# K and Q rounded in the second layer's quanta, loads six pairs ahead, joined visits from the ninth pair on

## The chip, the cores and the metric

One core of one Trainium2 chip. The metric is device time in microseconds (us) of one execution. A core has five engines that run their own instruction queues in order and wait for each other through semaphores: TensorE (PE, with its weight loads PEld), VectorE (DVE), ScalarE (ACT), GpSimd (POOL) and SyncE (SP, which here only issues transfers).

## The reference

Attention with a window of 32 positions to each side and 8 global positions, over 8 batches x 8 heads x 576 positions x 64; then a two-layer network on the 4608 tokens of width 512.

```python
scores = scale * np.matmul(q, k.transpose(0, 1, 3, 2))
mask = np.abs(pos[:, None] - pos[None, :]) <= window
mask = mask | is_global[:, None] | is_global[None, :]
scores = np.where(mask, scores, -1000000000.0)
attn = softmax(scores)
x = np.matmul(attn, v)            # heads side by side: 4608 x 512
h = x @ w_in                      # 512 -> 2048
r = np.maximum(h, 0.0)
g = s * (r * r) + b
out = g @ w_out                   # 2048 -> 512
```

## The kernel before, in words

**Pairs.** Two heads of one batch are a pair; there are 32, four to a batch. A pair's scores come in two halves, g = 0 and 1, each a call of `qk(p, g)` (line 623): six matmuls of K's transposed tile `kt` against Q's transposed tile `qt` into PSUM (`pss`, or `psw` in the second pool), an exponential on ScalarE (`em`, line 641), and a multiplication with the mask on VectorE one slot later (line 642). `pvq` (line 644) multiplies the `em` halves of two pairs with V (`po`); `norm_steps` turns `po` into `xt`, the input of the network: `ln` and `rep` on ScalarE, `gs`, `tot`, `xg` and `xt` on VectorE. `scatter` copies the global rows with POOL.

**The network in quanta.** `moe_quanta` (line 738) is a generator over 9 tiles of 512 tokens. A tile has 16 quanta of the first layer (4 matmuls `psh`, then a relu `r` on ScalarE and, one slot later, its square `g` on VectorE) and 16 of the second (4 matmuls `pso` each; after four quanta VectorE stores 128 rows). Ahead of the first tile, `lead()` takes the first steps of it: halves of four quanta that need two heads only.

**Slots.** `run_pair` (line 856) gives each pair 8 slots s = 0..7. In a slot it issues the pieces of attention that a rule puts there, runs what the slot before left over (`prev`), then the list `extra` of the slot (filled by `at(s, f, ...)` in the loop of line 1111), and ends with `Q(nq[s])`, as a rule one quantum. The queues of all engines are written in this order. From pair 13 on the phase is steady: the second layer runs from slot 4 of a batch's last pair (hp = 3) to slot 3 of the next batch's second pair (hp = 1), the first layer from there on.

**Visits.** Up to pair 11 (`JOIN`) the two halves of a pair come at two slots of their own. From pair 11 on there is one visit in slot 3 (`VISIT`): `visit(p)` (line 847) computes the second half of pair p and the first half of pair p + 1 together; the latter uses two PSUM banks (`ps_w`, tile `psw`) that belong between visits to the ring `ps_n` of the network. `BANKS` says by the slot since the visit which of the two rings a quantum's bank comes from. For pair 11 itself the rules of both kinds hold: the first half in slot 0, the visit in slot 3, and in slot 4 the unjoined second half.

**How K and Q get ready.** From pair 8 on, K is loaded by SP in float32 (`natk`, four slots, `load_nat`), rounded to bfloat16 by ScalarE (`round_k`, line 234, `natb`) and turned by a transposing transfer that SP issues (`turn_k`, line 293, tile `kt`, three buffers). `put_kq(p, (0,))` (line 546) then copies the 8 global columns into `kt` on VectorE (line 552). Q is loaded (`load_q`, `natq`) and rounded (`round_q`, line 276, `sixq`); up to pair 17 TensorE transposes it (`trans_b`, `pst`) and VectorE takes it out, from pair 18 (`QTURN`) on `turn_q` does; `put_kq(p, (1,))` copies its global columns. SP's queue holds the loads of K, Q and V (V up to pair 15; later POOL) and the transposes, in the order of the program, and a transfer waits for the landing of the eighth before it.

**When.** The loop of line 1111 sets the slots: loads of K and Q five pairs ahead; the roundings of two pairs in each last and each first pair of a batch (`todo`, lines 1160 to 1174, slots 1, 3, 5 and 7); `turn_k(p + 2)` at the start of a pair; `put_kq(p + 1, (0,))` in slot 2 (line 1132), one slot before the visit.

Of the kernel before, what the change touches and what calls it, by code (L numbers as in the profile page):

```python
# [40 lines left out]
NSIX = 8  # L41
NSIXQ = 13
JOIN = 11
# [3 lines left out]
VISIT = 3  # L47
BANKS = "mmnnmnmm"
# [36 lines left out]
def kernel(  # L85
# [471 lines left out]
    def trans(t, p):  # L557
        if p < 5 or (t == "k" and p > 5):
            ps = bank("pst").bitcast(BF16)[:, 0:LQ]
        elif t == "k" or p == JOIN + 1:  # L560
# [41 lines left out]
    def trans_b(p, later=later):  # L602
        ps = trans("q", p)

        def evac():
# [12 lines left out]
            if p >= 6:  # L618
                put_kq(p, (1,) if p >= NSIX else (0, 1))
# [118 lines left out]
    def moe_quanta():  # L738
        for t in range(NTOK // 512):
# [116 lines left out]
    def run_pair(p, nq, extra):  # L856
# [4 lines left out]
        for s in range(8) if p > 4 else range(NCH, 8):  # L861
            prev, later[:] = list(later), []
            now = []
            joined = p > JOIN
            if p >= JOIN:
                when[0] = (s - VISIT) % 8
# [6 lines left out]
            if joined and s in (4, 5):  # L873
                step()
                if s == 5 and hp == 0:
                    later.append(lambda: scatter(bi - 1))
            if s < NCH:
                if s in (2, 3) and not joined:
                    step()
                if s == 4 and hp == 0 and bi > 1 and not joined:  # L880
# [16 lines left out]
            elif s == 5:  # L897
                if p == 4:
                    cast_v(A, 5)
                if 4 < p < JOIN:  # L900
                    trans_b(p + 1, now)
            if s == 4 and 4 < p < NSIX - 1:
                trans_a(p + 1, now)
            if s in (5, 6) and not joined:
# [3 lines left out]
            if p > 4 and s == (VISIT if joined else 4 if p % 2 else 1):  # L908
# [157 lines left out]
    lead()  # L1066
    qk(4, 1)
# [43 lines left out]
    for p in range(4, NPAIR):  # L1111
# [13 lines left out]
        if p in (JOIN, JOIN + 1):  # L1125
            nq[(1, VISIT)[p - JOIN]] = 0
        if p > 7 and hp != 3 and p + 2 < NPAIR:
            turn_k(p + 2)
        if p >= JOIN and p + 1 < NPAIR:
            if p + 1 >= QTURN:  # L1130
                at(1, put_kq, p + 1, (1,))
            at(2, put_kq, p + 1, (0,))
        elif NSIX <= p + 1 < NPAIR:
            at(7, put_kq, p + 1, (0,))
        for j in {4: (8,), 5: (9,), 6: (10,), 7: (11, 12)}.get(p, (p + 5,)):
            if j < NPAIR:
                if j in (10, 11, 12):
# [110 lines left out]
```

## Time and profile before

| | us |
|---|---|
| median of three runs | 347.2 (345.22 to 347.98) |
| the profiled execution, its own time | 344.5 |
| its span, first to last instruction | 342.9 |
| PE busy in the span | 325.4 |
| DVE, ACT, POOL busy | 205.9, 201.0, 113.8 |
[...]

The profile follows one execution on the core. The busy time of an engine is the union of its instructions; idle time of TensorE is what lies between. A row of a timeline gives the start, the length, engine, line, operation, tile written <- tile read, shape, and in brackets the idle time of that engine before it and the instruction that ended it. Bank and buffer numbers are left out of the names.

### The profile page before, as it was taken

The numbers are of one execution on the slowest core, as the hardware profiler recorded it, in microseconds if no ns is written. First come the engines' busy times: TensorE is split into PE (matmuls) and PEld (weight loads), VectorE is DVE, ScalarE is ACT, GpSimd is POOL, SyncE is SP. The second block draws the span as 40 slices with busy tenths as digits, with TensorE's granted clock in tenths as the row PEclk, the third lists the DMA queues.
The fourth block names the chain that finished last, engine by engine and source line by source line (L and its number), as shares of the span: only waits on it lengthen the run. The fifth ranks groups of instructions, "written<-read, shape, count | busy, mean of one in ns | idle before, by whom it ended". The sixth has DMA issues, their size and how long they took to land.

```text
span 342.9 us, 8737 instructions
## 1 busy us (share of the span) xinstructions
PE 325.4 (95%) x3370; PEld 168.3 (49%) x3370; DVE 205.9 (60%) x541; ACT 201.0 (59%) x338; POOL 113.8 (33%) x220
## 2 busy tenths in 40 slices
PE   7898899899999999999899989998999999999995
PEld 4555343444444444477544444444466544444444
DVE  5489677555758688856665666566656534423422
ACT  3555787647795578567855885588358505503600
POOL 7741842143001415372368306831670030000000
PEclk9999999999999999999999999999999999999999
DMA  9999999989998999999499999993960011011012
GB/s 154 193 211 196 209 206 192 221 173 250 164 158 149 217 190 176 194 175 161 81 227 211 194 136 223 201 189 83 210 124 2 2 68 56 0 62 61 3 44 78
DMA packets 133533, 50.08 MB, mean 146 GB/s; under 512 B 122124, under 2 KB 128588, under 8 KB 133484
## 3 DMA queue, kind: packets, MB, share of 16 engines
q1 hardware_dynamic: 101346, 28.33, 48.7%
q0 software_dynamic: 31792, 20.77, 35.7%
q8 instruction: 26, 0.43, 0.5%
q10 hardware_dynamic: 354, 0.43, 0.4%
q14 instruction: 15, 0.12, 0.1%
HBM read 42.35 MB, written 9.44 MB: 151 GB/s over the span
## 4 chain that ended last, share of the span: by engine, by line
PE 73%; ACT 5%; DMA 5%; issue 5%; POOL 3%; SPq 3%; DVE 3%; POOLq 1%; ACTq 0%
PE pso L787 35%; PE psh L753 29%; PE po L658 5%; ACT r L775 3%; SPq L224 3%; DMA win_t<-in_moe_w_in_dram 2%; PE pss L634 2%; DVE g L778 2%; PE psw L634 1%; DMA natq<-in_q_dram 1%; DMA kt<-natb 1%; ACT em L641 1%; POOL sixq L197 1%; ACT sixq L278 1%; POOL gf L392 1%
## 5 line engine op out<-in xcount | busy, mean ns | idle before, releaser
L753 PE MATMUL psh<-xt,win_t 128*128 128x512 bf16 (+2 forms) x704 | 131.1, 341 | 1.0 <-POOL xt L730 0.6
L787 PE MATMUL pso<-wout_t,g 128*128 128x512 bf16 (+1 forms) x592 | 129.8, 374 | 0.0
L775 ACT ACTIVATE r<-psh 128x512 bf16<-128x512 f32 x144 | 85.1, 599 | 59.4 <-PE psh L753 58.8
L753 PEld LDWEIGHTS <-win_t 128*128 128x128 bf16 x704 | 63.4, 98 | 58.5 <-issue 2.1
L778 DVE TENSOR_TENSOR g<-r 128x512 bf16<-128x512 bf16 x144 | 60.4, 422 | 47.5 <-ACT r L775 46.1
L787 PEld LDWEIGHTS <-g 128*128 128x128 bf16 x592 | 55.9, 98 | 62.8
L641 ACT ACTIVATE em<-pss 128x840 bf16<-128x840 f32 (+1 forms) x42 | 37.3, 888 | 49.5 <-PE pss L634 49.4
L642 DVE TENSOR_TENSOR em<-em,mask 128x840 bf16<-128x840 bf16 (+1 forms) x65 | 39.2, 609 | 34.2 <-ACT em L641 33.9
L730 POOL COPY xt<-xg 128x4 bf16 (+1 forms) x72 | 16.8, 233 | 58.8 <-DVE xt L705 55.0
L807 DVE SCALAR_TENSOR_TENSOR osb<-pso,sb,bias_row 128x512 f32<-128x512 f32 (+1 forms) x25 | 18.2, 728 | 30.1 <-PE pso L787 30.0
L224 POOL DMA_DIRECT2D vring<-in_v_dram x33 | 29.5, 897 | 10.8 <-PE po L658 10.0
L705 DVE TENSOR_TENSOR xt<-po,rep 128x480 bf16<-128x480 f32 (+2 forms) x60 | 24.5, 449 | 2.1 <-ACT rep L715 2.1
L634 PEld LDWEIGHTS <-kt 64*128 64x128 bf16 x390 | 12.1, 99 | 26.4 <-issue 14.1
L811 POOL DMA_DIRECT2D out_dram<-osb x16 | 9.0, 565 | 32.1 <-DVE osb L807 25.3
L634 PE MATMUL pss<-qt,kt 64*128 64x192 bf16 (+4 forms) x252 | 16.1, 239 | 2.9 <-DVE qt L938 1.4
L641 ACT ACTIVATE em<-psw 128x904 bf16<-128x904 f32 x20 | 18.5, 926 | 0.0
L658 PE MATMUL po<-em,vring 128*32 128x160 bf16 (+3 forms) x840 | 17.7, 221 | 0.5 <-issue 0.5
L235 ACT CAST natb<-natk 128x640 bf16<-128x640 f32 x24 | 17.3, 722 | 0.5 <-DMA natk<-in_k_dram 0.5
L712 ACT ACTIVATE ln<-po 128x324 f32<-128x324 f32 (+1 forms) x30 | 12.9, 430 | 5.8 <-PE po L658 5.8
L715 ACT ACTIVATE rep<-ln 128x324 f32<-128x324 f32 (+1 forms) x32 | 14.7, 460 | 0.5
L658 PEld LDWEIGHTS <-vring 128*32 128x32 bf16 x896 | 13.7, 98 | 0.8 <-issue 0.8
L950 PE MATMUL psf<-dummy 128*128 128x512 bf16 x21 | 10.3, 573 | 1.8 <-DVE dummy L320 1.4
(125 smaller groups left out, 246.9 us busy)
## 6 DMA issues: line engine op xcount, KB each, us to landing
natk<-in_k_dram SPq DMA_DIRECT2D x47, 150.0 KB
natv<-in_v_dram SPq DMA_DIRECT2D x28, 150.0 KB
natq<-in_q_dram SPq DMA_DIRECT2D x55, 75.0 KB
wst<-in_moe_w_out_dram POOLq DMA_DIRECT2D x8, 512.0 KB, 5.0
out_dram<-osb POOLq DMA_DIRECT2D x16, 256.0 KB, 2.3
vring<-in_v_dram POOLq DMA_DIRECT2D x31, 75.0 KB, 5.3
out_dram<-osbh POOLq DMA_DIRECT2D x9, 256.0 KB, 2.8
win_t<-in_moe_w_in_dram POOLq DMA_DIRECT2D x4, 512.0 KB
```

What stands on the lines that cost most here:

```text
L224: eng.dma_start(out=dst[r : r + rows, n, c : c + nch, hh], in_=bass.AP(tensor=src[t].tensor, offset=o + c * KC * D, ap=[[D, rows], [KC * D ...
L235: nc.scalar.copy(out=natb[:, p % NV].rearrange("p (c h d) -> p c h d", c=NCH, h=2), in_=natk[:, p % NV],)
L634: nc.tensor.matmul(ps[:, hh, at : at + hi - lo], ktile[p][r, P * c : P * c + P], qbufs[p % 3][r, lo:hi], start=at == 0, stop=at + hi - lo ...
L641: nc.scalar.activation(em[:], ps[:, :, 0:n], AF.Exp, scale=SCALE)
L642: later.append(lambda: nc.vector.tensor_mul(em[:], em[:], masks[g]))
L658: nc.tensor.matmul(po[DH * j : DH * j + DH, a : a + n], view(vring[:, p % NVR, c, hh, part - 1 :], [2, DH]) if part else onesb[:], emt[(p, ...
L705: nc.vector.tensor_tensor(out=view(xt[:, 2 * g, x0 + t0 :], [NXT, 2], [w, runs], [1, w]), in0=view(po[:, STEP[blk] + col :], [STEP[blk], 2 ...
L753: nc.tensor.matmul(psh[:, d0 : d0 + n], win_t[:, a, f * P : f * P + P], xt[:, a, x0 : x0 + n], start=(a == 0 and j == 0), stop=(a == 3), s ...
L775: nc.scalar.activation(r[:], psh, AF.Relu)
L778: later.append(lambda g=g, r=r: nc.vector.tensor_mul(g[:], r[:], r[:]))
L787: nc.tensor.matmul(pso[:, 0:nn], gl[f][:, u * P : u * P + P], wout_t[:, f, n0 : n0 + nn], start=(f == 0), stop=(f == 15),)
L807: nc.vector.scalar_tensor_tensor(out=osb[:, 0:nn], in0=pso[:, 0:nn], scalar=s_bc, in1=bias_row[:, n0 : n0 + nn], op0=OP.mult, op1=OP.add,)
```

## The change

The table `VISITS` gives each visit's slot, counted over all pairs: slot 7 in pairs 8 and 9, 6 in pair 10, 5 in pair 11, 3 from pair 12 on. `JOIN` becomes 8, and at pair 8 only the first half is computed on its own. Everything that hung on slot 3 now hangs on the distance to a visit: the transposes of Q three slots ahead, the copies of the global columns two slots ahead, the normalization one and two slots behind, the bank of a quantum. The roundings, transposes and loads follow tables by pair.

```diff
-JOIN = 11
+JOIN = 8
-VISIT = 3
-BANKS = "mmnnmnmm"
+VISITS = {8 * p + {8: 7, 9: 7, 10: 6, 11: 5}.get(p, 3): p for p in range(JOIN, NPAIR)}
...
-            pool = rings[int(name == "psg" or BANKS[when[0]] == "n")]
+            ago = min((when[0] - x for x in VISITS if x <= when[0]), default=8)
+            left = min((x - when[0] for x in VISITS if x > when[0]), default=8)
+            near = ago < 2 or left < 3 or ago == 4
+            pool = rings[int(name == "psg" or not near)]
...
                     into(led[f], f, (0, 1))
-                    if f % 2:
-                        yield
+                    yield
...
-            if p >= JOIN and s == VISIT:
+            if at in VISITS:
                 visit(p)
-            elif not joined and p > 4 and s in ((0, 4) if p % 2 else (1, 3)):
+            elif 4 < p < JOIN and s in ((0, 4) if p % 2 else (1, 3)) or (p, s) == (JOIN, 1):
                 qk(p, int(s > 1))
-            if p >= JOIN and s == 0 and p + 1 < QTURN:
-                trans_b(p + 1, now)
+            j = VISITS.get(at + 3, NPAIR) + 1
+            if j < QTURN:
+                trans_b(j, now)
...
     qk(4, 0)
     lead()
+    lead()
     qk(4, 1)
...
+    k_out = turned(trans_a, 5)
+    lead()
     q_out = turned(trans_b, 5)
-    k_out = turned(trans_a, 5)
+    k_out()
     q_out()
-    k_out()
...
-        if p >= JOIN and p + 1 < NPAIR:
-            if p + 1 >= QTURN:
-                at(1, put_kq, p + 1, (1,))
-            at(2, put_kq, p + 1, (0,))
...
+        for s in range(8):
+            j = VISITS.get(8 * p + s + 2, NPAIR) + 1
+            if j < NPAIR:
+                at(s, put_kq, j, (0, 1) if j >= QTURN else (0,))
+        if p + 1 == NSIX:
+            at(7, put_kq, NSIX, (0, 1))
+        for j in range(p + 1, min(p + 7, NPAIR)):
+            x = {
+                10: (6, 1), 11: (7, 4), 12: (7, 5), 17: (12, 0), 18: (13, 0), 19: (14, 0),
+                20: (14, 4),
+            }.get(j, (j - 5 if j < 17 else j - 6, 0))
...
-            todo = {8: (11,), 9: (12,)}.get(
-                p, {0: (p + 3, p + 4), 3: (p + 2, p + 3)}.get(hp, ())
-            )
-            for i, j in enumerate(todo):
-                if j < NPAIR:
-                    x = 4 if p in (8, 9) else 4 * i
-                    at(1 + x, round_k, j)
...
+                d, k_at, q_at = ((4, 6, 7), (4, 0, 2), (3, 4, 6), (3, 0, 2))[j % 4]
+                k_at = {
+                    8: (6, 4), 9: (7, 1), 10: (7, 5), 11: (8, 5), 12: (9, 5), 13: (10, 5),
+                    17: (13, 6),
+                }.get(j, (j - d, k_at))
...
+                t_at = {
+                    8: (6, 5), 9: (7, 3), 10: (7, 7), 11: (8, 7), 12: (9, 7), 13: (10, 7),
+                    14: (11, 6),
+                }.get(j, (j - 3, 5))
...
         elif p == 7:
-            at(3, steps[1])
+            at(4, steps[1])
```

What the tables move is seen in the queues. ScalarE, the first-layer stretch at pair 19 (`r` relus, `natb` and `sixq` the roundings of pair 21, `em` the visit's two exponentials), before:

```order
L775 ACTIVATE r<-psh 128x512
L715 ACTIVATE rep<-ln 128x292
L775 ACTIVATE r<-psh 128x512 x4
L235 CAST natb<-natk 128x640
L278 CAST sixq<-natq 128x640
L775 ACTIVATE r<-psh 128x512 x2
L641 ACTIVATE em_3364<-pss 128x840
L641 ACTIVATE em_3377<-psw 128x904
```

and in the changed kernel at the same place:

```order
L777 ACTIVATE r<-psh 128x512
L718 ACTIVATE rep<-ln 128x292
L777 ACTIVATE r<-psh 128x512 x6
L644 ACTIVATE em_3387<-pss 128x840
L644 ACTIVATE em_3400<-psw 128x904
```

The two casts have left the stretch; they stand two pairs earlier, in the second layer, between two visits.

VectorE at the same place (`g` squares, `qt<-gqt` and `kt<-gkt` the copies of global columns for pair 20), before:

```order
L778 TENSOR_TENSOR g_3322<-r 128x512
L552 COPY qt_119<-gqt_120 128x5x8
L778 TENSOR_TENSOR g_3340<-r 128x512
L552 COPY kt<-gkt 128x5x8
L1107 TENSOR_TENSOR osbh<-osbh,bias_row 128x512
L778 TENSOR_TENSOR g_3356<-r 128x512
L642 TENSOR_TENSOR em_3364<-em_3364,mask_454 128x840
```

and changed:

```order
L780 TENSOR_TENSOR g_3347<-r 128x512
L554 COPY kt<-gkt 128x5x8
L554 COPY qt_119<-gqt_120 128x5x8
L780 TENSOR_TENSOR g_3364<-r 128x512
L1115 TENSOR_TENSOR osbh<-osbh,bias_row 128x512
L780 TENSOR_TENSOR g_3379<-r 128x512
L645 TENSOR_TENSOR em_3387<-em_3387,mask_454 128x840
```

The copy of `kt` has moved ahead of one square.

ScalarE at the visit of pair 11 (`em`: three halves before, of which the third repeats the first), before:

```order
L641 ACTIVATE em_2024<-pss 128x840
L641 ACTIVATE em_2037<-psw 128x904
L284 CAST sixq<-natq 120x640
L641 ACTIVATE em_2059<-pss 128x840
L310 CAST vring<-natv 128x640
```

and changed:

```order
L312 CAST vring<-natv 128x640
L237 CAST natb<-natk 128x640
L644 ACTIVATE em_2063<-pss 128x840
L644 ACTIVATE em_2076<-psw 128x904
L715 ACTIVATE ln<-po 128x324
```

One exponential less, and the casts of V stand ahead of the visit.

## Rows read from the trace of the kernel before

**Rows 1.** The page: busy us, share of the span and instructions of each engine.
```profile
PE 325.4 (95%) x3370; PEld 168.3 (49%) x3370; DVE 205.9 (60%) x541; ACT 201.0 (59%) x338; POOL 113.8 (33%) x220
```

**Rows 2.** Stretches: length, then PE, PEld, DVE, ACT, POOL busy (instructions), clock, DMA, GB/s.
```profile
66.00:104.80 38.80, 37.05 (x381) 17.49 (x377) 24.00 (x61) 26.82 (x45) 6.95 (x14) 1.00 1.07 186
104.80:260.00 155.20, 151.69 (x1679) 80.22 (x1682) 103.81 (x268) 104.63 (x178) 69.12 (x121) 1.00 1.10 172
```

**Rows 3.** Timeline of PE at the visit of pair 19.
```profile
164.44 0.35 PE L634 MATMUL pss<-qt,kt 64*128 64x92 bf16 x6
165.73 0.37 PE L634 MATMUL psw<-qt,kt 64*128 64x160 bf16 x6 [0.94 <-DVE kt L552]
```

**Rows 4.** Timeline of ACT ahead of the same visit.
```profile
163.29 0.72 ACT L235 CAST natb<-natk 128x640 bf16<-128x640 f32 x1
163.90 0.73 ACT L278 CAST sixq<-natq 128x640 bf16<-128x640 f32 x1
164.53 1.08 ACT L775 ACTIVATE r<-psh 128x512 bf16<-128x512 f32 x2
```

**Rows 5.** Timeline of DVE ahead of the same visit.
```profile
165.16 0.42 DVE L778 TENSOR_TENSOR g<-r 128x512 bf16<-128x512 bf16 x1 [1.22 <-ACT r L775]
165.50 0.17 DVE L552 COPY kt<-gkt 128x40 bf16<-128x40 bf16 x1
```

**Rows 6.** Groups, PE, 104.8 to 259 us: count | busy us, mean ns | idle before, releaser.
```profile
L634 PE MATMUL psw<-qt,kt 64*128 64x160 bf16 (+2 forms) x108 | 6.5, 227 | 3.4 <-DVE kt L552 3.2
```

**Rows 7.** Timeline of PE at pairs 11 and 12.
```profile
97.43 0.36 PE L634 MATMUL pss<-qt,kt 64*128 64x92 bf16 x6 [0.47 <-ACT em L641]
97.72 0.39 PE L658 MATMUL po<-em,onesb 128*32 128x160 bf16 x12
...
104.85 0.36 PE L634 MATMUL pss<-qt,kt 64*128 64x92 bf16 x6
...
105.34 0.37 PE L658 MATMUL po<-em,onesb 128*32 128x92 bf16 x12
```

**Rows 8.** Waits of PE, 66 to 104.8 us: us in total, times, longest.
```profile
PE pss L634 <- DVE kt L552: 0.6, 2, 0.4
...
PE psw L634 <- DVE kt L552: 0.2, 1, 0.2
```

**Rows 9.** The page's groups: weight loads of all halves of scores.
```profile
L634 PEld LDWEIGHTS <-kt 64*128 64x128 bf16 x390 | 12.1, 99 | 26.4 <-issue 14.1
```

**Rows 10.** Timeline of PE, pairs 7 and 8.
```profile
58.77 0.25 PE L514 MATMUL psg<-ident,gb 64*64 64x64 bf16 x4 [0.77 <-DVE gb L506]
...
61.90 0.42 PE L575 MATMUL pst<-ident,sixq 96*128 96x96 bf16 x6 [0.90 <-ACT em L641]
...
65.87 0.37 PE L634 MATMUL pss<-qt,kt 64*128 64x160 bf16 x6
...
66.85 1.90 PE L787 MATMUL pso<-wout_t,g 128*128 128x512 bf16 x8
68.68 0.36 PE L634 MATMUL pss<-qt,kt 64*128 64x92 bf16 x6
68.97 1.25 PE L787 MATMUL pso<-wout_t,g 128*128 128x512 bf16 x5
```

**Rows 11.** Timeline of SP's queue: issues of loads and transposing transfers.
```profile
44.65 4.03 SPq L264 DMA_DIRECT2D natq<-in_q_dram  x1
...
61.48 2.78 SPq L295 DMA_TRANSPOSE kt<-natb  x2
...
98.21 3.11 SPq L295 DMA_TRANSPOSE kt<-natb  x1
...
137.94 1.35 SPq L224 DMA_DIRECT2D natk<-in_k_dram  x2
```

**Rows 12.** Timeline of DVE at the copy for pair 8.
```profile
65.43 0.39 DVE L552 COPY kt<-gkt 128x40 bf16<-128x40 bf16 x1 [0.16 <-DMA kt<-natb]
```

**Rows 13.** Timeline of PE near the end: one second layer without attention.
```profile
297.62 13.98 PE L787 MATMUL pso<-wout_t,g 128*128 128x512 bf16 x64
```

More of the change, by code (lines that the diff above doesn't have):

```diff
@@ L559, in trans @@
             ps = bank("pst").bitcast(BF16)[:, 0:LQ]
-        elif t == "k" or p == JOIN + 1:
+        elif t == "k":
             ps = rings[-1].tile([P, DM], FP32, tag="moe", name="pst")[:].bitcast(BF16)[:, 0:LQ]
@@ L618, in evac @@
             if p >= 6:
-                put_kq(p, (1,) if p >= NSIX else (0, 1))
+                if p != NSIX:
+                    put_kq(p, (1,) if p > NSIX else (0, 1))
         later.append(evac)
@@ L863, in run_pair @@
             now = []
-            joined = p > JOIN
+            at = 8 * p + s
             if p >= JOIN:
-                when[0] = (s - VISIT) % 8
-            if p >= JOIN and s == VISIT:
+                when[0] = at
+            if at in VISITS:
                 visit(p)
-            elif not joined and p > 4 and s in ((0, 4) if p % 2 else (1, 3)):
+            elif 4 < p < JOIN and s in ((0, 4) if p % 2 else (1, 3)) or (p, s) == (JOIN, 1):
                 qk(p, int(s > 1))
-            if p >= JOIN and s == 0 and p + 1 < QTURN:
-                trans_b(p + 1, now)
[L873 to L876, printed above, removed]
+            j = VISITS.get(at + 3, NPAIR) + 1
+            if j < QTURN:
+                trans_b(j, now)
+            for x in (1, 2):
+                if VISITS.get(at - x, 0) > JOIN:
+                    step()
+                    if x == 2 and VISITS[at - x] % 4 == 0:
+                        later.append(lambda: scatter(bi - 1))
             if s < NCH:
-                if s in (2, 3) and not joined:
+                if s in (2, 3) and p <= JOIN:
                     step()
-                if s == 4 and hp == 0 and bi > 1 and not joined:
+                if (p, s) == (JOIN, 4):
                     later.append(lambda: scatter(bi - 1))
@@ L899, in run_pair @@
                     cast_v(A, 5)
-                if 4 < p < JOIN:
+                if 4 < p < JOIN - 1:
                     trans_b(p + 1, now)
+            if (p, s) == (JOIN - 1, 6):
+                trans_b(p + 1, now)
             if s == 4 and 4 < p < NSIX - 1:
                 trans_a(p + 1, now)
-            if s in (5, 6) and not joined:
+            if s in (5, 6) and p < JOIN:
                 step()
@@ L907, in run_pair @@
                 f()
-            if p > 4 and s == (VISIT if joined else 4 if p % 2 else 1):
+            if VISITS.get(at, 0) > JOIN or 4 < p <= JOIN and s == (4 if p % 2 else 1):
                 put_out(p // 2 if p % 2 else p // 2 - 1, 1 - p % 2)
@@ L1157 @@
             at(6, gather, (p + 5) // 8)
[L1158 to L1180 removed]
+        for s in range(8):
+            for j in range(p + 1, min(p + 5, NPAIR)):
+                d, k_at, q_at = ((4, 6, 7), (4, 0, 2), (3, 4, 6), (3, 0, 2))[j % 4]
[3 more added lines that the diff above has]
+                }.get(j, (j - d, k_at))
+                q_at = {
+                    8: (6, 6), 9: (7, 3), 10: (7, 7), 11: (8, 7), 12: (9, 7), 13: (11, 2),
+                    17: (13, 7),
+                }.get(j, (j - d, q_at))
+                t_at = {
+                    8: (6, 5), 9: (7, 3), 10: (7, 7), 11: (8, 7), 12: (9, 7), 13: (10, 7),
+                    14: (11, 6),
+                }.get(j, (j - 3, 5))
+                if j >= NSIX and k_at == (p, s):
+                    at(s, round_k, j)
+                if j >= NSIX and q_at == (p, s):
+                    at(s, round_q, j)
+                if j >= NSIX and t_at == (p, s):
+                    at(s, turn_k, j)
+                if j >= QTURN and (j - 3, 7) == (p, s):
+                    at(s, turn_q, j)
         if p == 7:
```

42 lines of the change are left out of this document (9 added, 33 removed).

## The prediction

> **What bounds the kernel now.** I read the page's busy shares first, then the stretches by stage, then the waits inside each stretch, and last the timelines of single waits. TensorE is busy 95% of the span [rows 1], so the change can win only what TensorE idles or does needlessly. The stretches say where that is [rows 2]: from 104.8 to 260 us TensorE is busy 151.69 of 155.20 us, 3.5 us idle; from 66 to 104.8 us it is busy 37.05 of 38.80, 1.75 idle. After 260 us only matmuls of the two layers remain, and the change does not reach them.
>
> The 3.5 us have one cause. In all 18 visits of that stretch that join two pairs, the only idle time stands before `psw`, 3.4 us in all, 3.2 of them ended by VectorE's copy `kt` of line 552 [rows 6]. The visit of pair 19 shows how it comes about. ScalarE rounds K and Q of pair 21 (`natb`, `sixq`, 0.72 and 0.73 us) in the middle of a first-layer stretch, and two relus `r` start only at 164.53 [rows 4]. VectorE's square `g` waits 1.22 us for its relu and runs at 165.16; the small copy `kt`, though its transfer landed long before, stands behind it and runs at 165.50 [rows 5]. TensorE has issued `pss` at 164.44 and idles 0.94 us before `psw` at 165.73 [rows 3]. So it is a wait by order, not by data. Pairs 15, 23 and 27 have the same one, since before the change every fourth pair's casts stand there; what is left is small change at the other first-layer visits.
>
> **The change, part by part.** The sum is made against the profiled execution, 344.5 us (span 342.9). The median of the three runs shown is 347.2, so that execution is 2.7 us faster than the median; I apply the difference to the median.
>
> (a) Rounding and the copies. From pair 21 on, every fourth pair's two casts leave the first layer for slots 0 and 2 of the second layer, two pairs earlier, where no relu is queued on ScalarE. In those slots the casts stand ahead of `em` of the same visit only; `em`'s reader is the mask multiply, then `po` at the next visit, a whole pair later, so that cover holds. Pair 17's casts remain among relus, but five quanta ahead of the next visit instead of just before it. The copy `kt` moves one slot ahead, so it waits for the relu of one quantum earlier; a quantum is 4 matmuls of 13.98/64 = 0.218 us [rows 13], 0.87 us, nearly the whole 0.94 of the wait in [rows 3] even if nothing else changed. Both together remove 3.4 us; I keep 0.2 for what may stay: -3.2 (bounds -3.4 and 0).
>
> (b) The first joined pair. Before, pair 11 computes its second half twice: once in the visit of slot 3, once in slot 4, where the unjoined rule still holds. The page shows it: 390 weight loads on line 634 at 6 a half make 65 halves for 32 pairs [rows 9]. The second copy is the `pss` at 97.43, with 0.47 us idle before it (its PSUM is read by ScalarE's `em`) and 0.29 until `po` [rows 7]. It goes: 0.76, with the switch into it 0.8: -0.8.
>
> (c) Between 66 and 96 us `kt` copies stop `pss` twice (0.6) and `psw` once (0.2) [rows 8], at pairs 10, 11 and 12, which now are halves of joined visits whose copies come two slots ahead: -0.8 (bounds -0.8 and 0).
>
> (d) Pairs 8, 9 and 10 are joined too. A half on its own costs 68.97 - 68.68 = 0.29 us, and the run ahead of it 66.85 to 68.68 = 1.83 where 8 matmuls take 1.75, so 0.08 more [rows 10, 13]; two halves in a joined visit take 105.34 - 104.85 = 0.49 instead of 0.58 [rows 7]. That is 0.17 a pair: -0.5 (bounds -0.6 and 0).
>
> (e) What does not come. At 58.77 and 61.90 TensorE idles 0.77 and 0.90 us [rows 10], and the change takes away the first (the small transposes `psg` move one slot later) and perhaps 0.2 of the second. But at 65.87 the next half needs `kt` of pair 8, and VectorE's copy of it starts at 65.43, 0.16 us after it was free, because the transposing transfer lands then [rows 12]. That transfer was issued at 61.48 [rows 11], behind the same loads as in the changed kernel: the loads of pair 9 are only moved ahead of a V load, the bytes ahead of it are equal. So TensorE comes about 1.5 us earlier and waits 1.5 us longer; the reordered half quanta at 36 us (0.2 us) vanish in the same wait. Q's copy of pair 8 now stands behind `kt`'s there: +0.1.
>
> [...] The trace has 65.43 - 61.48 = 3.95 us from issue to use [rows 11, 12], because older loads are still in the queue; I go by the rows.
>
> (f) New waits. Joined visits of pairs 8 to 11 ask for `kt` and `qt` earlier than before, and ScalarE has relus, two casts and two `em` per visit there. The trace shows no such visit in the first layer before 95 us; the nearest row, `psw` of pair 12, waits 0.2 [rows 8]. Four visits at 0.1: +0.4. Bounds: 0, and 4 x 0.94 = 3.8, the worst of [rows 3].
>
> Loads six pairs ahead move no bytes and feed casts that already found their data; I cost them at nothing. Their cover is the transfer queue: if it fails, the third rival holds. The moved order of PSUM banks gives the same banks at eight slots between visits, also nothing.
>
> Sum: -3.2 - 0.8 - 0.8 - 0.5 + 0.1 + 0.4 = -4.8. The profiled execution becomes 339.7, the median 342.4.
>
> **Rivals.** First: the early joined visits wait for transfers. The transpose of pair 13 began to issue at 98.21 and was issued at 101.32 [rows 11]. Pair 8's was used 2.6 us after its own issue ended (half of the 2.78 for two, from 61.48, is 62.87; 65.43) [rows 11, 12], so pair 13's serves at 103.9. By the sum, the visit that wants it comes at 104.85 [rows 7] less the 0.8, 0.8 and 0.5 of (b) to (d), plus 0.1 and 0.4: 103.25, its `psw` 0.2 later. If the transfer is as late as before, 0.6 us of waiting with the copy; the same at pairs 11 and 12 makes 1.8: -3.0, median 344.2. For it: the SP queue is in use without a pause there. Against: the changed kernel issues these transposes two or three slots earlier. Second: the first-layer waits shrink only by half, because ScalarE's relu is late for another reason than the casts: 1.6 of (a) and 0.4 of (c) are lost, -2.8, 344.4. Against it: in rows 4 nothing but the two casts stands between relus.
>
> Third, slower: loads six pairs ahead keep the SP queue full after 105 us. A load then takes 4 us to issue, as the one at 44.65 did, not 0.7 as the two at 137.94 do [rows 11]. A transpose leads its copy by 12 slots, some 12 us with the visit, and needs 3.95; from 8 us of backlog on, that is two such loads, VectorE waits in order at the copy and TensorE behind it. An excess of 0.6 us at the 15 visits from pair 16 on costs 9 us: -4.8 + 9 = +4.2, median 351.4. Against it: the rows after 105 us are short, and the bytes are the same. [...]
>
> Fourth, faster: the transpose of pair 8 lands when TensorE wants it, and (e) gives 1.6 more: -6.4, median 340.8.
>
> **How the numbers follow.** Forecast 0.60, first rival 0.16, second 0.13, third 0.05, fourth 0.06. The forecast alone spans -6.3 to -3.3, medians of 340.9 to 343.9; the three runs of before lie 2.0 below to 0.8 above their median, so I go to 339.2 below, and to 345.6 above to hold the first two rivals. 1% is 3.5 us, about what a measurement of this kernel can tell; faster by more than that is a median under 343.7: the fourth rival, 0.55 of the forecast and a little of the others, 0.62. Within 1%: 0.33. Slower: the third rival, 0.05.
>
> **What would show it.** Right: no idle time before `psw` after 105 us; ScalarE's casts between `em` and the second layer's end only; 384 weight loads on line 634's successor; `psw` of pair 9 near 73 us; `pss` of pair 8 still near 65.9 with 1 us or more of waiting for `kt`. Wrong: waits on `kt` copies released by transfers after 66 us, or `psh` waiting for ScalarE.

## The result, and the profile after

The changed kernel's median is 338.44 us (six runs, 337.43 to 339.38) against 347.06 for the kernel before (six runs): ratio 0.976, 95% interval 0.9725 to 0.9794, 8.6 us less. Forecast were 342.4, with a range from 339.2 to 345.6: the direction holds, the gain is larger than the range allowed. The execution profiled took 338.75 us (span 337.1), 5.75 less than the one profiled before, 344.5.

The gain was not the same each time it was timed. In two later sessions, on two chips and each time beside the kernel before, the changed kernel had 339.57 against 344.69 (ratio 0.984, 95% interval 0.975 to 0.994) and 341.71 against 346.42 (0.989, 0.984 to 0.994). Ratios and intervals are taken over fast runs alone, medians over all; three of the eleven runs behind 346.42 were slow, over 1.5% above the fastest. Why the gains differ is half of what follows.

The page's first part for the changed kernel, to be held against [rows 1]:

```profile
PE 317.5 (94%) x3324; PEld 168.3 (50%) x3364; DVE 205.7 (61%) x540; ACT 199.6 (59%) x337; POOL 113.7 (34%) x220
```

There are 3364 weight loads and only 3324 matmuls: some matmul records are missing here, so TensorE's busy time is too low and gaps of 0.05 and 0.16 us that end with "issue" are no stops. What is missing from the work itself is six of 3370 weight loads, one exponential and one mask multiplication: the repeated half of pair 11. The page's group of weight loads for the scores says the same, 384 for the 390 of [rows 9]:

```profile
L637 PEld LDWEIGHTS <-kt 64*128 64x128 bf16 x384 | 12.1, 99 | 18.1 <-issue 13.6
```

The stretches of [rows 2], now from pair 8's first half to pair 12's visit, and from there to 258 us (columns as there):

```profile
68.30:103.70 35.40, 34.92 (x370) 17.65 (x375) 23.66 (x60) 26.21 (x45) 7.23 (x14) 1.00 1.06 181
103.70:258.00 154.30, 152.22 (x1698) 83.00 (x1715) 106.37 (x274) 107.49 (x183) 69.46 (x121) 1.00 1.13 175
```

The idle time before `psw`, 3.4 us in [rows 6], is all but gone; the group of the changed kernel from 103.7 to 258 us:

```profile
L637 PE MATMUL psw<-qt,kt 64*128 64x160 bf16 (+2 forms) x114 | 6.8, 225 | 0.1
```

How it went shows at the visit of pair 19. TensorE's timeline (for [rows 3]):

```profile
162.84 0.36 PE L637 MATMUL pss<-qt,kt 64*128 64x92 bf16 x6
163.03 0.36 PE L637 MATMUL psw<-qt,kt 64*128 64x160 bf16 x6
163.32 0.38 PE L661 MATMUL po<-em,onesb 128*32 128x160 bf16 x12
```

VectorE's (for [rows 5]):

```profile
161.83 0.42 DVE L780 TENSOR_TENSOR g<-r 128x512 bf16<-128x512 bf16 x1 [0.45 <-ACT r L777]
162.17 0.17 DVE L554 COPY kt<-gkt 128x40 bf16<-128x40 bf16 x1
162.25 0.17 DVE L554 COPY qt<-gqt 128x40 bf16<-128x40 bf16 x1
162.70 0.43 DVE L780 TENSOR_TENSOR g<-r 128x512 bf16<-128x512 bf16 x1 [0.28 <-ACT r L777]
```

and ScalarE's (for [rows 4]):

```profile
162.07 0.60 ACT L777 ACTIVATE r<-psh 128x512 bf16<-128x512 f32 x1 [0.28 <-PE psh L756]
162.94 0.60 ACT L777 ACTIVATE r<-psh 128x512 bf16<-128x512 f32 x1 [0.28 <-PE psh L756]
163.44 0.86 ACT L644 ACTIVATE em<-pss 128x840 bf16<-128x840 f32 x1
```

`psw` follows `pss` by 0.19 us where it was 1.29; the copy `kt` is done 0.7 us before it is wanted, and no cast stands between the relus. The waits of [rows 8] are gone too: between 66 and 104 us no wait of TensorE for a copy is left.

Ahead of pair 8 the profiled execution lost time. ScalarE's cast of pair 5's V waited for its transfer, all relus behind it:

```profile
42.28 0.72 ACT L312 CAST vring<-natk 128x640 bf16<-128x640 f32 x1 [4.33 <-DMA natk<-in_v_dram]
```

and TensorE with them; it reached pair 8 at 68.27, 2.4 us later than before [rows 10], and found `kt` there:

```profile
43.55 3.27 PE L756 MATMUL psh<-xt,win_t 128*128 128x512 bf16 x8 [3.55 <-ACT r L777]
...
68.27 0.37 PE L637 MATMUL pss<-qt,kt 64*128 64x160 bf16 x6
```

So I cut every profile at three rows of TensorE's timeline, `pss` of pair 8's first half, `pss` of pair 12's visit and the end of the last matmul. Before: 65.87, 104.85 and 339.27 (the last row is 14.02 long from 325.25). Three stretches come out, and 5.2 us around them that are the same in all. All numbers in us:

| profile of | to pair 8 | pair 8 to 12 | from pair 12 | time |
|---|---|---|---|---|
| before | 65.9 | 38.98 | 234.4 | 344.5 |
| before, second profile | 68.2 | 38.09 | 234.8 | 346.2 |
| before, repeat removed | 67.4 | 37.27 | 236.1 | 346.0 |
| before, copy a slot earlier | 67.0 | 38.10 | 230.0 | 340.4 |
| changed | 68.3 | 35.44 | 229.8 | 338.8 |
| changed, second profile | 69.2 | 37.27 | 229.6 | 341.2 |
| changed, third profile | 69.0 | 36.16 | 229.6 | 339.9 |
| changed, fourth profile | 67.3 | 37.12 | 229.5 | 339.1 |
| changed, casts back, first | 69.7 | 36.56 | 233.4 | 345.1 |
| changed, casts back, second | 66.1 | 36.84 | 229.5 | 337.7 |
| changed, copy a slot later | 71.6 | 35.44 | 231.9 | 344.1 |
| changed, five pairs ahead | 67.9 | 36.29 | 229.6 | 338.9 |
| changed, joined from 11 | 70.5 | 38.59 | 231.8 | 346.1 |

Where nothing was edited that bears on it, the last stretch is steady to 0.4 us from profile to profile, with one exception, and the change is worth 4.6 to 5.2 in it. The exception is "joined from 11", which is 2.2 longer there by a single stop of 2.13 us at pair 17's visit: VectorE had waited 1.67 us for a transfer of the network's weights, and the copies of global columns stood behind. The middle stretch gives 0.8 to 2.7, by luck. The first gives nothing that shows.

### The profile page after: what moved, and what is told of

It is laid out like the page before. It is cut to its first block, busy times and chain, and to the rows that moved or that the text cites. A ratio compares the mean times of both kernels' runs of the same rounds, so it can differ in the third digit from the quotient of the medians.

```text
span 337.1 us, 8682 instructions
## 1 busy us (share of the span) xinstructions
PE 317.5 (94%) x3324; PEld 168.3 (50%) x3364; DVE 205.7 (61%) x540; ACT 199.6 (59%) x337; POOL 113.7 (34%) x220
## 4 chain that ended last, share of the span: by engine, by line
PE 78%; DMA 10%; SPq 5%; issue 3%; DVE 2%; ACT 0%; POOL 0%; POOLq 0%; DVEq 0%; ACTq 0%
PE psh L756 35%; PE pso L789 33%; PE po L661 5%; SPq L226 5%; DMA natk<-in_v_dram 5%; DMA wst<-in_moe_w_out_dram 4%; PE pss L637 2%; DMA sixk<-in_k_dram 2%; PE psw L637 1%; DVE wsum L1104 1%; PE pst L583 0%; DVE xt L708 0%; PE pst L577 0%; ACT r L777 0%; DVE g L780 0%
## 5 line engine op out<-in xcount | busy, mean ns | idle before, releaser
L756 PE MATMUL psh<-xt,win_t 128*128 128x512 bf16 (+4 forms) x688 | 131.1, 342 | 5.9 <-ACT r L777 3.6
L789 PE MATMUL pso<-wout_t,g 128*128 128x512 bf16 (+1 forms) x573 | 126.4, 373 | 2.4 <-issue 2.1
L644 ACT ACTIVATE em<-pss 128x840 bf16<-128x840 f32 (+1 forms) x38 | 33.6, 884 | 47.1 <-PE pss L637 47.1
L645 DVE TENSOR_TENSOR em<-em,mask 128x904 bf16<-128x904 bf16 x64 | 38.6, 611 | 32.9 <-ACT em L644 32.6
L733 POOL COPY xt<-xg 128x4 bf16 (+1 forms) x72 | 17.8, 247 | 58.1 <-DVE xt L708 54.3
L644 ACT ACTIVATE em<-psw 128x904 bf16<-128x904 f32 x23 | 21.3, 927 | 0.0
L661 PE MATMUL po<-em,vring 128*32 128x160 bf16 (+3 forms) x840 | 17.0, 218 | 0.0
L637 PE MATMUL pss<-qt,kt 64*128 64x192 bf16 (+4 forms) x228 | 14.8, 242 | 1.7 <-DVE qt L944 0.9
L661 PE MATMUL po<-em,onesb 128*32 128x192 bf16 (+2 forms) x360 | 11.3, 232 | 0.8 <-DVE xt L708 0.7
```

The costliest lines, as they stand in the source:

```text
L637: nc.tensor.matmul(ps[:, hh, at : at + hi - lo], ktile[p][r, P * c : P * c + P], qbufs[p % 3][r, lo:hi], start=at == 0, stop=at + hi - lo ...
L644: nc.scalar.activation(em[:], ps[:, :, 0:n], AF.Exp, scale=SCALE)
L645: later.append(lambda: nc.vector.tensor_mul(em[:], em[:], masks[g]))
L661: nc.tensor.matmul(po[DH * j : DH * j + DH, a : a + n], view(vring[:, p % NVR, c, hh, part - 1 :], [2, DH]) if part else onesb[:], emt[(p, ...
L733: nc.gpsimd.tensor_copy(out=xt[:, h, S * (bi % NX) : S * (bi % NX) + S][:, :, ds(greg_p[i], 1)], in_=xgs[bi][:, h, i : i + 1],)
L756: nc.tensor.matmul(psh[:, d0 : d0 + n], win_t[:, a, f * P : f * P + P], xt[:, a, x0 : x0 + n], start=(a == 0 and j == 0), stop=(a == 3), s ...
```

## Experiments

### Second profiles, and the cast that waited

The two kernels as they are, and both with ScalarE's cast of pair 5's V three slots later:

```diff
-                if p == 4:
-                    cast_v(A, 5)
...
+            if (p, s) == (5, 2):
+                cast_v(A, 5)
```

Before, second profile:

> The kernel before, unchanged, looked at a second time. Theory (the execution profiled first was a lucky one): its 344.5 us is 2.6 below the median of six because pair 5's second V transfer landed at 39.2 us there; in a common execution it lands near 42 as in the changed kernel, ScalarE's cast waits 3 to 4 us for it and TensorE idles 2 to 3 us near 40 us, so the span is 344.5 to 346 (time 346 to 347.6). Rival (the 2.6 us are spread over the run, as fetch pauses of TensorE or a lower clock): no wait of more than 1.5 us near 40 us, the stretch from 66 to 260 us longer.

Changed, second profile:

> The changed kernel, unchanged, looked at a second time. Theory: from the visit of pair 12 to the last matmul 229.8 us again (229.6 to 230.0), since nothing waits there; what varies lies ahead of the first half of pair 8 (68.3 us in the first profile; 66.5 to 68.6 here, with the idle time near 40 us between 2 and 4 us). Rival: the stretch behind pair 12 varies by over 0.5 us.

Changed, with the later cast:

> The changed kernel with ScalarE's cast of pair 5's V moved three slots later, to slot 2 of pair 5, and its global rows behind it. Theory: the 3.55 us that TensorE idles at 40 us go; the first half of pair 8 then waits again for its transposing transfer (landed at 65.94, copy at 66.0 to 66.4), so pss of pair 8 comes near 66.5 instead of 68.3 and the time falls by 1.5 to 2.2, median 336.2 to 336.9. Rival (the cast only shows a general lateness of transfers, another one stops TensorE as long): under 0.5 us gained, median 338 or more.

Before, with the later cast:

> The kernel before with the same cast moved three slots later. Theory (common executions of before also idle at 40 us for this cast, unlike the one profiled): it gains about the distance of the median from the profiled execution, 1.5 to 2.6 us, median 344.4 to 345.6. Rival (the V wait is something that only the changed kernel has, and before's median is above its profile for other reasons): under 0.5 us, median 346.6 or more.

Measured: 346.2, 341.22; 339.59 (four runs); 345.36 (ten) against 346.93, ratio 0.997 (0.9935 to 1.0008). In the kernel before, the later cast takes 1.6 us off the median, but the interval includes no change at all. In the changed kernel no gain shows (338.44 in the first session): TensorE stops at 64.6 for 2.2 us instead, for the copies of pair 8's `kt` and `qt`. So the theory falls there, and the rival holds: another transfer stops TensorE. The second profiles show that in most executions the long stop is for pair 3's V, not for pair 5's as the first theory had it. Before, at 34.14 (TensorE's timeline):

```profile
34.14 0.57 PE L658 MATMUL po<-em,onesb 128*32 128x160 bf16 x12 [5.31 <-DVE xt L705]
```

and in the third profile of the changed kernel, VectorE, whose cast of that V stands ahead of the `xt` that TensorE wants:

```profile
33.19 0.49 DVE L312 CAST vring<-natv 128x640 bf16<-128x640 f32 x1 [6.54 <-DMA natv<-in_v_dram]
```

In the two executions profiled first, this stop was 0.2 and 0.7 us; in eleven of thirteen later ones with these loads on SP it was 3 to 10. It also costs clock. TensorE's stretches in that third profile, before the stop, in it and behind it (columns as in [rows 2], the granted clock ahead of the DMA share):

```profile
25.00:29.40 4.40, 4.23 (x97) 2.61 (x96) 1.65 (x4) 1.94 (x5) 0.00 (x0) 1.00 1.14 204
29.40:35.41 6.01, 0.00 (x1) 0.00 (x2) 2.22 (x7) 0.00 (x0) 0.00 (x0) 0.69 1.21 191
35.41:38.60 3.19, 3.19 (x87) 2.24 (x88) 2.91 (x14) 0.92 (x2) 1.33 (x7) 0.52 1.08 197
```

Over the whole run the thirteen have a mean granted clock of 0.985 to 0.995 on record, which does not tell where it was lower. Behind the 3.55 us of the changed kernel's first profile it is 0.55 from 43.55 to 46.80: read in half microseconds 0.50 from 44.0 to 47.0, 0.69 in the next and 1.00 from 47.5 to 54. In the first profile of before, whose stop here is 0.2 us, it is 1.00 in every microsecond from 28 to 66.

Of the changed kernel's second profile, the rival (the stretch behind pair 12 varies by over 0.5 us) failed: 229.60 against 229.84. Pair 8 came at 69.2, later than the theory had.

The second profile of the changed kernel has a stop more, at the visit of pair 10, which computes the first half of pair 11 (TensorE):

```profile
91.05 0.35 PE L637 MATMUL pss<-qt,kt 64*128 64x92 bf16 x6
93.13 0.37 PE L637 MATMUL psw<-qt,kt 64*128 64x160 bf16 x6 [1.73 <-DVE kt L554]
```

VectorE's copy for it waits for the transposing transfer:

```profile
92.90 0.17 DVE L554 COPY kt<-gkt 128x40 bf16<-128x40 bf16 x1 [2.05 <-DMA kt<-natb]
```

which SP had begun to issue 9.6 us earlier:

```profile
83.33 1.78 SPq L297 DMA_TRANSPOSE kt<-natb  x1
```

That is the first rival of the prediction, at pair 11, which it names beside 13. It came in two of four profiles of the changed kernel (1.73 and 0.62) and in most of its variants.

### One part undone, one part alone

The casts of pairs 21, 25 and 29 and their transposes back in the first layer:

```diff
+                if j in (21, 25, 29):
+                    k_at, q_at, t_at = (j - 2, 1), (j - 2, 1), (j - 2, 3)
```

> The changed kernel with the two casts of pairs 21, 25 and 29 and their transposes put back where they stood before, in slots 1 and 3 of the first layer, the copies of global columns staying two slots ahead of the visit. Read: the stretch from pss of pair 12's visit to the last matmul, 229.6 to 229.8 us in three profiles of changed kernels, 234.4 to 234.9 in three of before. Theory (the copy was late only because it stood behind the square that the casts delay; one slot earlier it stands ahead of it): 229.6 to 230.2, no wait over 0.15 us before psw. Rival (the casts delay the earlier square as well, so moving them was needed): three waits of 0.5 to 1.0 us at pairs 19, 23 and 27, each costing 0.17 more than shown, 231.8 to 233.3.

Measured: 233.41, with stops of 2.04 and 1.37 us at `psh`. That says nothing about the casts: they now wait for a newer load into the buffer that they read. So once more with these loads behind them:

```diff
+            if j in (25, 29):
+                x = (j - 6, 2)
```

> The same as the experiment that put the casts of pairs 21, 25 and 29 back, but with the loads of pairs 25 and 29 issued two slots later, behind the casts of 21 and 25 that read the same buffer (in the run before they stood ahead of these casts, so ScalarE waited 2.0 and 1.4 us for them and took the wrong keys). Stretch from pss of pair 12's visit to the last matmul, 229.6 to 229.8 in the changed kernel. Theory (the earlier copy alone passes by the late square): 229.6 to 230.2. Rival (the casts delay the earlier square or the quanta themselves): 231 to 233.3, with waits of psw on kt or of psh on r at pairs 19, 23 and 27.

Measured: 229.53, no wait before `psw`. The casts need not have moved.

The copy `kt` one slot later again, the casts where the change put them:

```diff
-            j = VISITS.get(8 * p + s + 2, NPAIR) + 1
+            j = VISITS.get(8 * p + s + (1 if p >= 12 else 2), NPAIR) + 1
```

> The changed kernel with the copy of kt's global columns one slot ahead of the visit again from pair 12 on, the casts where the change put them. Same stretch. Theory (a stop costs its idle time and 0.17 more; the small stops of before, 0.07 to 0.33 at pairs 14, 15, 22, 26 and 30, come back, and pairs 19, 23 and 27 get small ones of the same kind, 0.08): 230.9 to 231.9. Rival (moving the casts alone removed everything): 229.6 to 230.0, no wait before psw; other rival (the copy's place is all): 233.9 or more, the three waits of 0.95 back.

Measured: 231.86, at the top of the theory's range. The group of `psw` from 109 to 262 us:

```profile
L637 PE MATMUL psw<-qt,kt 64*128 64x160 bf16 (+2 forms) x108 | 6.6, 227 | 0.9 <-DVE kt L554 0.3
```

Eight small stops, 0.9 us idle together, cost 231.86 - 229.61 = 2.25 against the second and third profiles: 0.87 and 8 x 0.17 = 2.23. So the moved casts alone would have given about half of the gain.

And the kernel before with that one number changed:

```diff
-            at(2, put_kq, p + 1, (0,))
+            at(1, put_kq, p + 1, (0,))
```

> The kernel before with one number changed: the copy of kt's global columns in slot 1 instead of slot 2, two slots ahead of the visit, from pair 12 on. Stretch from pss of pair 12's visit to the last matmul, 234.4 to 234.9 in three profiles of before, 229.5 to 229.8 in six profiles of changed kernels with the copy there. Theory (where the copy stands is all of that gain; the moved casts and loads are worth nothing beside it): 229.5 to 230.2, and the time falls by 4.5 to 5.2. Rival (in the kernel before, with its loads and transposes, the casts also hold the earlier square): 231 to 233, the time falls by 2 to 3.5.

Measured: 230.01, and 340.2 us (four runs) against 344.69, ratio 0.986 (0.977 to 0.994). The changed kernel, on the same chip in the same session, had 339.57. VectorE at pair 19 in this kernel:

```profile
163.76 0.17 DVE L552 COPY qt<-gqt 128x40 bf16<-128x40 bf16 x1
163.84 0.16 DVE L552 COPY kt<-gkt 128x40 bf16<-128x40 bf16 x1
165.16 0.42 DVE L778 TENSOR_TENSOR g<-r 128x512 bf16<-128x512 bf16 x1 [1.15 <-ACT r L775]
```

and TensorE:

```profile
164.43 0.36 PE L634 MATMUL pss<-qt,kt 64*128 64x92 bf16 x6
164.62 0.36 PE L634 MATMUL psw<-qt,kt 64*128 64x160 bf16 x6
```

The casts still stand between the relus and the square still comes 1.15 us late. TensorE no longer depends on it: the copy has passed it.

The loads five pairs ahead again:

```diff
-                20: (14, 4),
-            }.get(j, (j - 5 if j < 17 else j - 6, 0))
+                20: (15, 0),
+            }.get(j, (j - 5, 0))
```

> The changed kernel with all loads of K and Q five pairs ahead, as before the change. Same stretch. Theory (the casts find their data either way): 229.6 to 229.9. Rival (the early casts of pairs 21, 25 and 29 need the sixth pair): ScalarE waits for natk there, relus come late, 230.5 or more.

Measured: 229.56. ScalarE's waits (us in total, times, longest) show that the sixth pair does what it should:

```profile
ACT sixq L280 <- DMA natq<-in_q_dram: 6.4, 3, 2.8
ACT natb L237 <- DMA natk<-in_k_dram: 1.9, 2, 1.4
```

but TensorE did not pay for it. Four of the five waits, 6.9 us, stand behind pair 12's visit, where the changed kernel has none; the stretch is as short as before, since in the second layer nothing that TensorE wants soon stands behind these casts. So the loads six pairs ahead were not needed either.

### The middle stretch

Joined visits from pair 11 on only (`JOIN = 11`, with the copies for pairs 9 to 11 in slot 7 and the steps of pair 11 as before the change):

> The changed kernel with joined visits from pair 11 on only, at its slot 5; pairs 8, 9 and 10 in two halves of their own, their copies in slot 7 of the pair before, as before the change. Read: the stretch from pss of pair 8's first half to pss of pair 12's visit, 35.4 in the changed kernel, 38.1 in two profiles of before (39.0 in the first). Theory (joining saves 0.17 a pair and lets the copies come two slots ahead, so that waits of 0.2 to 0.4 with 0.17 each go): 36.7 to 37.4, with two or three waits of pss on kt copies. Rival (what shortened it is the repeated half that went; joining brings nothing): 35.3 to 35.7.

The repeated half removed from the kernel before:

```diff
+            elif not joined and p > 4 and s in ((0, 4) if p % 2 else (1, 3)) and (p, s) != (JOIN, 4):
```

> The kernel before without the second computation of pair 11's second half (slot 4), nothing else changed. Same stretch as for the joined visits, 38.1 in two profiles of before. Theory: the half goes with its wait of 0.46 on ScalarE, its own 0.29 and 0.17 for the stop: 37.1 to 37.3. By the prediction's term, 0.8: 37.3. Rival (the next wait takes its place): over 37.7.

Measured: 38.59, more than the theory or the rival had, with two stops that neither had foreseen beside the one that the theory had. TensorE's waits in this kernel from 70 to 109 us:

```profile
PE pst L577 <- ACT em L644: 1.2, 1, 1.2
PE po L661 <- DMA vring<-gvall: 0.7, 1, 0.7
...
PE pss L637 <- DVE kt L554: 0.2, 1, 0.2
```

These three are 2.05 idle, 2.56 if each costs 0.17 more, as a stop at `psw` does; with the prediction's 0.5 for three unjoined pairs that makes 3.1 of the 3.15 by which it is longer than 35.44. Neither the 0.17 at `pst` and `po` nor the 0.5 is measured here, and the other steps were shaped for joined visits: this is no clean price of joining, and no run gives one.

Without the repeat the middle stretch is 37.27, 0.83 less than 38.10: the term of the prediction. But pair 12's visit came earlier and pair 13's transpose did not (VectorE, then TensorE):

```profile
106.32 0.18 DVE L552 COPY kt<-gkt 128x40 bf16<-128x40 bf16 x1 [2.90 <-DMA kt<-natb]
```

```profile
106.55 0.37 PE L634 MATMUL psw<-qt,kt 64*128 64x160 bf16 x6 [1.49 <-DVE kt L552]
```

In the kernel before, alone, this edit was paid back at the next visit in the one execution profiled.

### The first stretch: whose transfer comes first

SP loads V while POOL loads the network's weights. Pair 2's and 3's V moved into POOL's queue, just ahead of the weights:

```diff
-    for p in range(6):
+    for p in (0, 1, 4, 5):
         load_v(nc.sync, p)
...
+    load_v(nc.gpsimd, 2)
+    load_v(nc.gpsimd, 3)
     load_w_in(0)
```

> The changed kernel with the V loads of pairs 2 and 3 issued by POOL, in the queue of the network's weights and just ahead of them, not by SP. Read: the wait of VectorE for natv near 28 to 36 us (0.7 to 9.7 us of TensorE's time in eight profiles) and the time. Theory (what varies from run to run is the race of the two queues: the megabytes of w_in push the V loads back by up to 8 us): V lands by 25, the stop at po near 29 us is under 1 us, first half of pair 8 at 66 to 68.5, time 336.5 to 339.5 in every run. Rival (all transfers are late by the same amount, so the next one stops TensorE): the weights or pair 5's V land later by as much, no gain and the same spread.

The same with pair 10's loads behind the transpose of pair 8, and the later cast:

> As the run before, and pair 5's V cast three slots later, and the loads of pair 10 issued behind the transpose of pair 8 rather than ahead of it. Theory (ahead of pair 8 TensorE waits for two transfers, V of pair 5 and the transpose of pair 8, and each wait also costs slower clock behind it): both waits go, first half of pair 8 at 63.5 to 65.5 and the time 333.5 to 336.5. Rival (the stream of transfers up to 66 us is the bound whatever its order): first half of pair 8 at 66 or later, or a new wait at pairs 9 and 10, 337 or more.

Measured: 337.07 (four runs, 335.16 to 337.68) and 339.99, against 345.39 for before (ratios 0.973 and 0.985). The wait near 30 us is gone in both. The second edit brought pair 8 forward to 65.4 and paid with 2.55 us at pair 11 (middle stretch 39.45): its rival. With pair 13's loads (K, Q, V) behind the transpose of pair 11, alone and with that edit too:

```diff
-                10: (6, 1), 11: (7, 4), 12: (7, 5), 17: (12, 0),
+                10: (6, 1), 11: (7, 4), 12: (7, 5), 13: (9, 0), 17: (12, 0),
```

> The changed kernel with pair 2's and 3's V loads in POOL's queue, and the loads of pair 13 (K, Q, V) issued one pair later, behind the transpose of pair 11. Theory (psw of pair 11 waits in six of nine profiles of changed kernels because its transpose queues behind these 0.9 MB): no wait of psw near 88 us, stretch from pair 8's first half to pair 12's visit 35.4 to 35.8, time 335 to 337, 0.5 to 1.5 under the kernel with V alone moved. Rival (the backlog is not these loads): the wait stays at 0.5 us or more, or the next transposes, of pairs 12 and 13, come late.

> As the run before, and the loads of pair 10 issued behind the transpose of pair 8. Theory: both transposes come in time, first half of pair 8 at 64.5 to 65.5, middle stretch 35.4 to 36, time 333.5 to 335.5. Rival (the stream is the bound; what is pulled ahead at pair 8 is paid at pairs 9 to 12, as the run with pair 10's loads alone moved showed with 2.55 us at pair 11): middle stretch over 37.

The changed kernel beside them:

> The changed kernel once more, timed on the same chip as the next two. Theory: 337.4 to 341.2 as before, the spread being VectorE's wait for pair 3's V near 30 us (0 to 10 us) and the stop of pair 11's psw for its transpose near 90 us (0 to 1.9 us).

Measured: 337.84, 339.06 and 339.57 (four runs each, spreads of 2.7 to 5.6 us). `psw` waits no more for pair 11's transpose, but 1.69 for pair 12's at the next visit, and with both edits 1.44 there, ended by ScalarE's cast of a V: the rivals again. Reordering shifts this wait; it doesn't remove it. Last, the two that mattered, in five rounds on one chip:

> The changed kernel timed in more rounds beside the kernel before on one chip. Theory (its sure gain is 5.0 in the stretch from pair 12 on and 0.8 to 2.7 between pairs 8 and 12; ahead of pair 8 both kernels are at the mercy of the same transfers): 5 to 8.6 us under before, ratio 0.976 to 0.986. Rival (the first session's 8.6 is the rule): ratio 0.973 to 0.979.

> The changed kernel with pair 2's and 3's V loads in POOL's queue, beside the changed kernel on the same chip. Theory (the wait near 30 us, 0.7 to 9.7 us, goes, but half of it is paid at the transpose of pair 8): 1 to 2.5 us under the changed kernel, highest run lower too. Rival (all of it is paid later): within 0.7 of it.

Measured: 341.71 and 338.12 (six runs each), 346.42 for before: ratios 0.989 (0.984 to 0.994) and 0.977 (0.973 to 0.982). The gain of the changed kernel, 4.7, is below what its theory and its rival had. Moving two V loads into the other queue beats the changed kernel by 3.6 us here, more than expected, and every one of its runs lies under the median of the changed kernel. The changed kernel's fourth profile is of the fastest of its six runs (339.14), so the others' stops stay unseen; but their granted clock is on record, 0.984 to 0.995 over the run, against 0.993 to 1.00 with the V loads moved.

## Why the prediction was right and wrong

**(a) Rounding and copies, -3.2: right about the cause, wrong in size.** The step that failed is "Both together remove 3.4 us": the term measured 4.57 between the two profiled executions. The 3.4 is the idle time in front of `psw`; a stop there costs more. From `pss` of pair 19, at 164.44 before [rows 3] and 162.84 after, to `pss` of pair 20:

```profile
173.77 0.36 PE L634 MATMUL pss<-qt,kt 64*128 64x92 bf16 x6
171.07 0.36 PE L637 MATMUL pss<-qt,kt 64*128 64x92 bf16 x6
```

Between two visits that frame one stop, the kernels differ by 1.11 us at pair 19 (0.94 idle), by 1.13 at 23 and 27 (0.96), by 0.50 at 15 (0.33), by 0.25 at 14, 22, 26 and 30 (0.07 or 0.08). Each is the idle time and 0.17. It can be read in [rows 3] and their counterpart: `psw` starts 0.19 after `pss` when nothing waits, while the row of `pss` is 0.35 long; when `psw` must wait, these 0.16 are spent as "busy" before the idle time begins. Eight stops behind pair 12's visit make 3.50 + 8 x 0.17 = 4.86, less one of 0.13 + 0.17 that the changed kernel still has at 145.5: 4.56; the stretch became shorter by 234.41 - 229.84 = 4.57. Not every stop costs the 0.17: where the casts were put back first, 2.04 us idle before `psh` lengthened the way between two visits by 2.09, and 1.37 by 1.42. What makes up the 0.17 at `psw` no run here shows; I had not weighed it. (Pair 15's wait, which the prediction calls the same as pair 19's, is 0.33, not 0.94.)

Of the two causes named, only the copy's place was needed. The prediction had noted that the slot alone gives nearly the whole 0.94; the kernel before with that one slot moved has 230.0 in this stretch.

**(b) The repeated half, -0.8: right.** 0.83.

**(c) and (d), -0.8 and -0.5: right in kind, 0.5 short.** From 38.10 to 35.44 are 2.66, less 0.83 leaves 1.83 for 1.3; three stops that went, at 0.17 each, are the difference. What is left for joining is 0.54, near the forecast 0.5, but as a remainder only. In the first profile of before the stretch is 0.9 longer for a pause at 78.8 that ends with "issue" and that no other profile of before has, so between the two profiled executions it shrank by 3.54.

**(e) Nothing won ahead of pair 8: right, for a reason that is not fixed.** The wait for pair 8's `kt` at 66 us that the prediction asked for is absent in the profiled execution, since the stop of 3.55 us for pair 5's V came first and TensorE reached pair 8 2.4 us later than before; it is 1.81 in the fourth profile. Which of the transfers comes last differs from execution to execution, and TensorE pays for one of them. That older loads stood ahead of pair 8's transpose, as the prediction has it, the kernel before shows on POOL. This cast waits for a V whose loads SP issued from 60.44 to 61.38, just ahead of the transpose, and starts 0.4 us before VectorE's copy of `kt` [rows 12]:

```profile
65.06 0.72 POOL L310 CAST vring<-natv 128x640 bf16<-128x640 f32 x1 [2.75 <-DMA natv<-in_v_dram]
```

**(f) New waits, +0.4: the size is near on the mean, the form wrong.** Not 0.1 at each of four visits, but one stop at pair 11's first half that comes or does not: 0, 1.73, 0.62 and 0 in the four profiles, 0.6 on the mean. Its releaser is the transfer, as in the first rival.

The second rival (waits shrink by half) and the third (a full SP queue behind 105 us) are refuted by 229.5 to 229.8 in the last stretch. The fourth (its 1.6 are the 1.5 and the 0.1 of (e)) asks that pair 8's transpose be there when TensorE comes early. In three of four profiles it was there, but TensorE came at 68.3 to 69.2, after a longer stop elsewhere; in the fourth profile TensorE would have come at 65.5 and waited for it.

**The sum.** With stops at their price the steps give -4.6 and -2.7, -7.3 in place of -4.8, in an execution in which pair 11's transpose is in time and the clock stays full; 0.8 to 1.9 less where they do not. Taken from the median of 347.2, as the prediction does, -7.3 is 339.9, inside its range; 338.44 lies another 1.5 below. The first session measured 8.6, the others 5.1 and 4.7. I can account for 4.6 to 5.2 in the last stretch and 0.8 to 2.7 in the middle; the rest of the difference between sessions must lie ahead of pair 8, where profiles of the changed kernel run from 67.3 to 69.2 and of before from 65.9 to 68.2. That the first session's runs were lucky with the wait near 30 us, as its profiled one was, is likely: behind the two stops shown above the granted clock was 0.52 and 0.55, and the granted clock of the changed kernel's six runs there is 0.993 to 1.00 (mean 0.997), while in the ten runs of the two later sessions it is 0.983 to 0.995 (mean 0.990). By (1 - clock) x span, an estimate and at most, that is 2 us a run. The stops themselves are seen only in the profiled runs, so the share of luck in the 8.6 is not shown. The range was too narrow on this account: I knew that the profiled execution of before was 2.7 faster than its median, and did not ask where. (Nor is 339.2 what the prediction's own numbers give: 340.9 less the 2.0 of the spread is 338.9.)

## What to carry to other kernels

Price a stop of TensorE by the interval between the groups on either side of it, with the stop and without, not by the idle column alone: here eight small stops at `psw` weighed 4.86 us where the column had 3.50. Before moving the heavy work that delays an engine's queue, look whether the one small instruction that the bottleneck waits for can pass ahead of it. Where two queues load at the same time, try putting what is needed first into the same queue as the bulk, ahead of it, which was worth 3.6 us here; and profile several executions before trusting one of a stretch that waits for transfers.

## What the runs showed of the hardware that I had not expected

The same transfer was there in time in one execution and 5 us later in another. Pair 3's V, issued by SP before POOL's weights, was there for VectorE without a wait at 28.1 in the first profile of the changed kernel (the second of two casts that run from 27.74), and only at 33.2 in its third, after a wait of 6.54 us. Ahead of the weights in POOL's own queue it made VectorE wait in none of five profiles. How the two queues share the transfers these runs do not show.

A stop of 1.81 us was followed by a lower clock, as that of 6.01 us was. Behind the shorter one, at pair 8 in the fourth profile, the stretches show the granted clock (the column ahead of the DMA share) at 0.69 and 0.80 of full speed:

```profile
65.40:67.26 1.86, 0.05 (x1) 0.00 (x2) 0.31 (x2) 0.74 (x1) 0.72 (x1) 1.00 0.83 141
67.26:70.50 3.24, 3.08 (x51) 1.52 (x53) 1.19 (x2) 2.33 (x4) 0.00 (x0) 0.69 1.02 235
70.50:74.00 3.50, 3.50 (x19) 1.62 (x18) 1.18 (x5) 0.07 (x1) 0.00 (x0) 0.80 1.05 212
```

The eleven matmuls of the second layer behind it took 4.22 us, where they take 2.54 in the first profile: 1.7 us, as much as the stop itself. That is why this middle stretch is 37.1 without a wait. In the first profile with the V loads in POOL's queue, a stop of 2.01 us at the same place left the clock as it was:

```profile
64.40:66.46 2.06, 0.06 (x1) 0.00 (x1) 1.13 (x4) 0.89 (x2) 0.72 (x1) 1.00 0.97 149
66.46:69.70 3.24, 3.08 (x56) 1.80 (x58) 1.38 (x2) 2.36 (x4) 0.00 (x0) 1.00 1.02 232
```

What tells the two apart these runs do not say.
